# Weight preparation in a fused attention and MLP kernel: mixing pinned to a later place, splits without GpSimd, six evictions by ScalarE

## The chip, the cores and the metric

One core of one Trainium2 chip runs the whole program. The metric is the device time of one execution in microseconds (us), lower is better. A core has five engines with a queue of instructions each: TensorE (matmuls; loading weights overlaps them), VectorE, ScalarE, GpSimd and SyncE, which here only issues DMA transfers. An engine works through its queue in order: an instruction that waits holds up all that stand behind it.

## The reference

Sigmoid attention for 8 batches of 12 heads, 448 positions and 64 channels, then two matrix products with a bend between them:

```python
scores = scale * np.matmul(q, k.transpose(0, 1, 3, 2)) - np.log(S)
attn = 1.0 / (1.0 + np.exp(-scores))
x = (attn @ v), heads side by side        # 3584 x 768
h = x @ w_in                              # 768 x 2048
g = np.where(h >= 1, h, np.where(h <= -1, 0.0, (h + 1) ** 2 / 4))
out = g @ w_out                           # 2048 x 768
```

## The kernel before

**Numbers.** The weights arrive as 64-bit floats. `Weight.convert` turns each chunk of 128 rows (16 chunks for w_in, 16 for w_out) into float32: ScalarE takes the high words (L226), VectorE adds the low bits (L234, L235), one of the two finds the largest value. Once a group of 8 chunks is converted, `find_scale` (L251 and on) makes a power of two from its largest value, and `Weight.split` makes two half-precision tiles of each chunk: high (ScalarE, L266 or L270) and low, the rest (VectorE, L271, one instruction). For some chunks GpSimd makes the low tile with two instructions (L267, L268): for w_in those of chunks 8 to 15, asked for from the sixth chunk of batch 0's first product on (`POOL_FROM`), for w_out every sixth, chunks 1, 7 and 13 (`WOP`). The half-precision tiles of chunk f lie where the float32 values of chunk f - 1 lay, so the splits of a weight follow one another. Products of such pairs are three matmuls: high by high, high by low, low by high.

**Stages.** First comes batch 0's attention in float32, beside the conversion of w_in. Then batch 0's MLP: 48 units of its first product (`up`, L708, six matmuls of 448 columns to a unit, three units to a chunk of h), then 24 units of the first half of its second product (`downs(0, 0)`, L744: chunks 0 to 7 of w_out, evicted from PSUM by VectorE in L754 and stored to `part` in DRAM). Between the units stand the attention steps of batch 1 (30 steps to a batch, five to a pair of heads) and the conversion of w_out. Batch 1's MLP follows: 24 units of its first product, 24 of the second half of batch 0's second product (`downs(0, 1)`, evicted with `part` added in L750), 24 more of its first product, then 48 of its own second product: units 0 to 119. Attention steps of batch 2 are spread evenly over units 0 to 101 (`share`, `DW`); at unit 102 `start_blocks` and `finish_blocks` turn batch 2's attention into operands (L516 to L537).

From batch 2 on the first product is done with one level of Strassen-like blocks: seven products instead of eight (`up_blocks`, L674), which need sums and differences of blocks of w_in. `mix(i)` makes them for chunks i and i + 8, eight steps in all: VectorE adds the high and low tiles back together (two instructions in L618, tile `mixa`), forms four block sums (L622 to L625), ScalarE and VectorE split two rows of them (L631, L632, tile `mixs`), VectorE rescales the unmixed blocks (four instructions in L641, tile `mixp`), and SyncE stores both to `blocks` in DRAM (L635, L644), from where batches 2 to 7 load them as sets (L650). The three tiles of a step come from a pool of two buffers (`raww`), which w_out's raw words used before. The steps stand in the program at batch 1's units 8, 17, 27, 36, 46, 56, 65 and 75 (`MIX0`, `MIX1`).

The bend of a chunk of h (`bend`) is two instructions of ScalarE (L721, L724) and three of VectorE (L722, L723, L725); L721 and L723 read PSUM. An attention step writes scores to PSUM, ScalarE takes the sigmoid, and from pair 14 on its result is split into two half-precision tiles (ScalarE L451, VectorE L452).

**What sets the order.** The program is traced in the order of the Python code, and a planner with a model of the engines' times then orders each engine's queue: an instruction may be put ahead of earlier ones when its operands are ready in the model. `tc.keep_in_program_order(ins)` forbids this for one instruction: it is issued after the instruction traced just before it on the same engine. `tc.high_priority` raises priority. Semaphores are placed by the framework.

Of the kernel before, what the change touches and what calls it, by code (L numbers as in the profile page):

```python
# [18 lines left out]
AF = mybir.ActivationFunctionType  # L19
ALU = mybir.AluOpType  # L20
# [14 lines left out]
NA = 8  # L35
AHEAD = 2
# [5 lines left out]
B0 = 9  # L42
B1 = 66
GPOOL = 1
POOL_FROM = 6
SUMS = (), (0, 1, 2, 3, 4, 8, 9, 10, 11, 12)
BEHIND = (1, 3, 4, 6, 7, 8, 10, 12, 13, 14, 16, 18, 19, 21, 22, 24)
SUM_LAG = 4
# [5 lines left out]
SB = 2  # L54
QA = 17
QT = 3
WOP = 6
MIXP = 0
CORN = 10
TP = 1  # L60

DW = 8
MIX0 = 8
MIX1 = 85
Q_PRIO = 72

PM = 9
# [5 lines left out]
def sigmoid_attention_mlp(ctx: ExitStack, tc: tile.TileContext, first_qvk, qkv, w_in, w_out, out_t):  # L73
    nc = tc.nc
# [103 lines left out]
    class Weight:  # L178
# [79 lines left out]
            self.scale.append(s)  # L258
            self.inv.append(inv)

        def split(self, f, pool=False):
            if f >= NFC:
                return
            w, hi, lo, scale = self.f32(f), self.sb[:, f, 0, :], self.sb[:, f, 1, :], self.scale[f >= NA]
            if pool:
                nc.scalar.activation(hi, w, AF.Copy, scale=scale)  # L266
                nc.gpsimd.tensor_scalar(out=w, in0=w, scalar1=scale, scalar2=1.0, op0=ALU.mult, op1=ALU.mult)  # L267
                nc.gpsimd.tensor_tensor(out=lo, in0=w, in1=hi, op=ALU.subtract)  # L268
            else:
                nc.scalar.activation(hi, w, AF.Copy, scale=scale)  # L270
                nc.vector.scalar_tensor_tensor(  # L271
                    out=lo, in0=w, scalar=scale, in1=hi, op0=ALU.mult, op1=ALU.subtract
                )


    raws, maxes, ready, hls, sums = {}, {}, {}, {}, {}
# [335 lines left out]
    def mix(i):  # L612

        to, ratio, minus = mixed["to"], mixed["ratio"], mixed["minus"]
        f, g, H = i, i + NFC // 2, DM // 2
        a = raw_p.tile([P, 2 * DM], I32, tag="raww", name="mixa").bitcast(F32).rearrange("p (r n) -> p r n", r=2)
        for r, chunk in ((0, f), (1, g)):
            (nc.gpsimd if r < MIXP else nc.vector).tensor_tensor(  # L618
                out=a[:, r], in0=w_in_sb[:, chunk, 0, :], in1=w_in_sb[:, chunk, 1, :], op=ALU.add
            )  # L620
        a11, a12, a21, a22 = a[:, 0, :H], a[:, 0, H:], a[:, 1, :H], a[:, 1, H:]
        nc.vector.tensor_tensor(out=a22, in0=a21, in1=a22, op=ALU.add)  # L622
        nc.vector.scalar_tensor_tensor(out=a21, in0=a11, scalar=ratio, in1=a21, op0=ALU.mult, op1=ALU.subtract)
        nc.vector.scalar_tensor_tensor(out=a11, in0=a11, scalar=minus, in1=a22, op0=ALU.mult, op1=ALU.add)
        nc.vector.scalar_tensor_tensor(out=a12, in0=a12, scalar=ratio, in1=a11, op0=ALU.mult, op1=ALU.subtract)  # L625
        st = raw_p.tile([P, 2 * DM], I32, tag="raww", name="mixs").bitcast(F16)
        sv = st.rearrange("p (r t h n) -> p r t h n", r=2, t=2, h=2)
        for r in range(2):
            src = a[:, r].rearrange("p (t n) -> p t n", t=2)
            hi = sv[:, r, :, 0, :]  # L630
            nc.scalar.activation(hi, src, AF.Copy, scale=to[1])  # L631
            nc.vector.scalar_tensor_tensor(  # L632
                out=sv[:, r, :, 1, :], in0=src, scalar=to[1], in1=hi, op0=ALU.mult, op1=ALU.subtract
            )
        nc.sync.dma_start(out=blocks[i][:, 3 * DM :], in_=st)  # L635
        pl = raw_p.tile([P, 2 * DM], I32, tag="raww", name="mixp").bitcast(F16)[:, : 3 * DM]
        pv = pl.rearrange("p (t h n) -> p h t n", t=3, h=2)
        for t0, n, chunk, k in ((0, 2, f, 0), (2, 1, g, 1)):
            src = w_in_sb[:, chunk].rearrange("p h (t n) -> p h t n", t=2)[:, :, 2 - n :, :]
            for h in range(2):  # L640
                nc.vector.tensor_scalar(  # L641
                    out=pv[:, h, t0 : t0 + n, :], in0=src[:, h], scalar1=to[k], scalar2=None, op0=ALU.mult
                )
        nc.sync.dma_start(out=blocks[i][:, : 3 * DM], in_=pl)  # L644
# [84 lines left out]
    def down(b, m, u, k):  # L729

        lo, hi = (0, NFC) if k is None else (GROUPS[k].start, GROUPS[k].stop)
        if u == 0:
            hold["po"] = ps_mo.tile([P, 512], F32, tag="mo", name="po")
            hold["o"] = out_p.tile([P, S], F32, tag="o", name="o")
            if m == 0:
                hold["od"] = down_sc[b, k]()
            if k == 1:
                nc.sync.dma_start(out=hold["o"], in_=part[m])
        po, o = hold["po"], hold["o"]

        pair = (u, u + NFC // 2) if b >= SB else (lo + 2 * u, lo + 2 * u + 1)
        for f in pair:
            for wh, gh in ((0, 0), (0, 1), (1, 0)):
                nc.tensor.matmul(  # L744
                    po[:, :S], w_out_sb[:, f, wh, m * P : (m + 1) * P], ghl[:, f, gh, :],
                    start=f == lo and wh + gh == 0, stop=f == hi - 1 and wh == 1,
                )
        if u == (hi - lo) // 2 - 1:
            if k == 1:
                nc.vector.scalar_tensor_tensor(  # L750
                    out=o, in0=po[:, :S], scalar=hold["od"], in1=o, op0=ALU.mult, op1=ALU.add
                )
            else:
                nc.vector.tensor_scalar(out=o, in0=po[:, :S], scalar1=hold["od"], scalar2=None, op0=ALU.mult)  # L754
            dst = part[m] if k == 0 else out_t[m * P : (m + 1) * P, b * S : (b + 1) * S]
            nc.sync.dma_start(out=dst, in_=o)

# [87 lines left out]
    for u, unit in enumerate(units):  # L845
        while at < 2 * NPIECE and B0 + (at - NPIECE) * (B1 - B0) // NPIECE <= u:
            step(at)
            at += 1
        if wi.at < NFC + 1:
            convert(wi, NFC + 1)  # L850
            wi.find_scale()
            group_scales(0, inv_x, 1)
        f, r = divmod(u, NCC // 2)

        assert all(at >= NPC * (p + 1) or (f + 1) * S * 4 <= slot_of(p) * 3 * S * 4 for p in range(NP, NFULL)), u
        if r == 0 and f < NFC:
            wi.split(f + AHEAD, f >= POOL_FROM)
        if wo.at < NA + 1:
            convert(wo, min(NA + 1, (u + 1) * (NA + 1) // WO_A))
            if wo.at == NA + 1:  # L860
                wo.find_scale()
                split_at = 0
        elif wo.at < NFC + 1:
            convert(wo, min(NFC + 1, NA + 1 + (u + 1 - WO_A) * (NFC - NA) // (WO_B - WO_A)))
            if wo.at == NFC + 1:
                wo.find_scale()
                roots()
        if len(wo.scale):
            while split_at < min(NA, 2 * (u + 1 - WO_A)):
                wo.split(split_at, split_at % WOP == 1)  # L870
                split_at += 1
        unit()
    while at < 2 * NPIECE:
# [5 lines left out]
    for b in range(1, B):  # L879
        units = ups_blocks(b) + downs(b)  # L880
        last = len(units) - 96 + LAST
        if b == 1:
            mix_scales()
            units = ups(1, 0, NA) + downs(0, 1) + ups(1, NA, NFC) + downs(1)
            last = len(units) - LAST1
        first = at

        share = [DW if b < SB or u < len(units) - 48 else 8 for u in range(last)]
        share = [sum(share[:u]) / sum(share) for u in range(last + 1)]
        with ExitStack() as order:  # L890
            if b >= PM:
                order.enter_context(tc.manual_schedule(engines={mybir.EngineType.PE}))
            for u, unit in enumerate(units):
                while at < min(b + 2, B) * NPIECE and (at - first) < share[min(u + 1, last)] * NPIECE:
                    step(at)
                    at += 1
                if b == 1:
                    while split_at < min(NFC, NA + (u + 1) * (NFC - NA) // (NA * NCC // 2 - 2)):
                        wo.split(split_at, split_at % WOP == 1)
                        split_at += 1  # L900
                    while mixed_at < NFC // 2 and u >= MIX0 + mixed_at * (MIX1 - MIX0) // (NFC // 2):
                        mix(mixed_at)
                        mixed_at += 1
                if b + 1 < B and u == last:
                    begun = start_blocks()
                unit()
                if b + 1 < B and u == last:
                    inv_x = finish_blocks(*begun)
                    block_scales(b + 1, inv_x)
                if b == 1 and u == last - 2:  # L910
                    for n in range(3):
                        load_set(n)
# [39 lines left out]
```

## Time and profile before

| | us |
|---|---|
| median of 3 runs | 1179.65 |
| lowest, highest | 1177.72, 1180.30 |
| profiled execution | 1179.06 |
| its span, as the profile has it | 1177.3 |
| TensorE busy in the span | 1140.0 (97%) |
| VectorE busy | 826.9 (70%) |
| ScalarE busy | 699.9 (59%) |
| GpSimd busy | 321.1 (27%) |

The profile is of one execution. A row of the table by stretch gives, for a part of the span, the busy time and number of instructions of PE (TensorE's matmuls), PEld (its weight loads), DVE (VectorE), ACT (ScalarE) and POOL (GpSimd), then the clock that was granted to TensorE as a share of full speed, the DMA engines' share and GB/s. With a tile's name it counts the instructions of that tile alone. A row of the view of one source line gives the count, the shortest, median and longest duration in ns, and the first and last start in us. In the chain each row is a start, a time and what it was spent on. A wait is given as: who waited, for whom, us in total, times, longest. L618 is line 618 of the kernel. Busy time of TensorE is modelled from its pipeline, so "busy" means that matmuls were in flight.

### The profile page before, as it was taken

How to read it: one execution, taken by the hardware profiler on the slowest of the kernel's cores; microseconds unless marked ns; L12 is line 12 of the kernel's file. 1: busy time of each engine (PE TensorE's matmuls, PEld its weight loads, DVE VectorE, ACT ScalarE, POOL GpSimd, SP SyncE). 2: the span in 40 equal slices, each digit the busy share in tenths (PEclk: the TensorE clock that was granted, in tenths of full speed). 3: DMA queues.
4: the chain of work that ended last, by engine and by line, in shares of the span. 5: the costliest groups of instructions: out<-in, count | busy, mean ns of one | idle time of the engine just before them, and what ended most of it. 6: DMA issues, size and time to landing. Idle time of an engine off the chain costs nothing.

```text
span 1177.3 us, 20221 instructions
## 1 busy us (share of the span) xinstructions
PE 1140.0 (97%) x7662; PEld 668.5 (57%) x7662; DVE 826.9 (70%) x1758; ACT 699.9 (59%) x1162; POOL 321.1 (27%) x389
## 2 busy tenths in 40 slices
PE   8889988799999999999999999999999999999998
PEld 2234333344445786467854677457764677558954
DVE  6998997997935788368873689367873688736830
ACT  6986984675743686448764577546864486523410
POOL 0025010100341353425353236233533253310000
PEclk9999999999999999999999999999999999999999
DMA  9941643447421465215733166324652256302400
GB/s 358 376 164 62 207 134 138 154 159 245 160 67 55 142 201 204 72 57 166 262 131 92 57 229 200 126 64 143 205 198 67 62 166 213 118 25 101 151 16 32
DMA packets 58113, 170.01 MB, mean 144 GB/s; under 512 B 8608, under 2 KB 39840, under 8 KB 51872
## 3 DMA queue, kind: packets, MB, share of 16 engines
q1 hardware_dynamic: 56288, 159.29, 39.6%
q10 hardware_dynamic: 1728, 9.44, 2.3%
q8 instruction: 60, 0.98, 0.4%
q14 instruction: 37, 0.30, 0.1%
HBM read 126.94 MB, written 23.40 MB: 128 GB/s over the span
## 4 chain that ended last, share of the span: by engine, by line
PE 74%; DVE 6%; DMA 5%; ACT 1%; POOL 1%; issue 1%; SPq 0%; POOLq 0%; ACTq 0%
PE po L744 34%; PE ph L674 23%; PE pav L484 7%; PE psc L402 3%; PE ph L708 3%; PE psc L411 2%; DMA blocks<-mixs 2%; PE psc L397 2%; DMA w_in_sb<-blocks 1%; DVE mixs L632 1%; DMA raw<-qkv 1%; DMA blocks<-mixp 1%; DVE w_out_sb L271 1%; DVE mixa L618 1%; DMA w_out_sb<-w_out 0%
## 5 line engine op out<-in xcount | busy, mean ns | idle before, releaser
L744 PE MATMUL po<-ghl,w_out_sb 128*128 128x448 f16 x2304 | 446.2, 353 | 7.2 <-DVE w_out_sb L271 3.6
L744 PEld LDWEIGHTS <-w_out_sb 128*128 128x128 f16 x2304 | 222.2, 98 | 224.5 <-issue 13.5
L674 PE MATMUL ph<-w_in_sb 128*128 128x224 f16 x3024 | 307.7, 259 | 1.7 <-DMA w_in_sb<-blocks 1.3
L674 PEld LDWEIGHTS <-w_in_sb 128*128 128x128 f16 x3024 | 282.6, 98 | 30.6 <-issue 27.3
L452 DVE SCALAR_TENSOR_TENSOR ahl<-psc,ahl 128x896 f16<-128x896 f32 (+1 forms) x170 | 153.0, 900 | 112.4 <-ACT ahl L451 110.4
L443 ACT ACTIVATE psc<-psc,nls,sqk 128x896 f32<-128x896 f32 (+1 forms) x136 | 129.6, 974 | 114.9 <-PE psc L411 97.1
L364 POOL TENSOR_SCALAR raw<-raw,qkv_s 128x448 f32<-128x448 f32 (+1 forms) x93 | 70.8, 774 | 451.1 <-DVE qkv_i L138 352.1
L451 ACT ACTIVATE ahl<-psc 128x896 f16<-128x896 f32 (+1 forms) x170 | 127.1, 763 | 29.9 <-DVE ahl L452 28.8
L708 PE MATMUL ph<-xhl,w_in_sb 128*128 128x448 f16 x576 | 114.7, 357 | 3.4 <-DVE g L723 2.0
L328 ACT ACTIVATE dump<-raw 128x448 f16<-128x448 f32 (+1 forms) x105 | 62.0, 590 | 77.6 <-DMA raw<-qkv 76.7
L683 DVE TENSOR_TENSOR xhl<-ph,xhl 128x224 f32<-128x224 f32 x240 | 87.8, 383 | 26.0 <-PE ph L674 19.8
L484 PE MATMUL pav<-ahl,v 128*64 128x448 f16 x748 | 96.5, 362 | 0.0
L721 ACT ACTIVATE g<-xhl,hr,ihr 128x448 f32<-128x448 f32 x96 | 69.0, 755 | 43.2 <-DVE xhl L683 42.3
L724 ACT ACTIVATE ghl<-g 128x448 f16<-128x448 f32 x128 | 72.8, 574 | 35.5 <-DVE g L723 35.2
L725 DVE TENSOR_TENSOR ghl<-g,ghl 128x448 f16<-128x448 f32 x128 | 86.8, 686 | 7.9 <-ACT ghl L724 6.6
L708 PEld LDWEIGHTS <-w_in_sb 128*128 128x128 f16 x576 | 55.6, 99 | 64.1 <-issue 16.2
L722 DVE SCALAR_TENSOR_TENSOR g<-g,rk 128x448 f32<-128x448 f32 x112 | 81.8, 745 | 10.6 <-ACT g L721 10.4
L754 DVE TENSOR_SCALAR o<-po,od 128x448 f32<-128x448 f32 x48 | 32.5, 679 | 62.5 <-PE po L744 62.4
L402 PE MATMUL psc<-qk 128*128 128x448 f16 x252 | 66.3, 354 | 7.2 <-ACT a L440 3.6
L366 POOL TENSOR_TENSOR hl<-raw,hl 128x448 f16<-128x448 f32 x62 | 69.6, 1140 | 0.0
L723 DVE SCALAR_TENSOR_TENSOR g<-xhl,ihs,g 128x448 f32<-128x448 f32 x96 | 65.8, 703 | 0.3
L484 PEld LDWEIGHTS <-v 128*64 128x64 f16 x748 | 36.6, 109 | 38.7 <-issue 24.3
(156 smaller groups left out, 1142.5 us busy)
## 6 DMA issues: line engine op xcount, KB each, us to landing
w_in_sb<-blocks SPq DMA_DIRECT2D x48, 1344.0 KB, 6.5
raw<-qkv SPq DMA_DIRECT2D x34, 704.0 KB, 4.8
qk<-hl SPq DMA_DIRECT2D x320, 56.0 KB, 2.0
w_out_sb<-w_in SPq DMA_DIRECT2D x16, 768.0 KB, 11.1
out_t<-o SPq DMA_DIRECT2D x48, 224.0 KB, 1.9
blocks<-mixs SPq DMA_DIRECT2D x8, 768.0 KB, 3.6
w_out_sb<-w_out ACTq DMA_DIRECT2D x6, 768.0 KB, 5.0
raww<-w_out ACTq DMA_DIRECT2D x6, 768.0 KB, 5.0
```

Source lines behind the costliest of these rows:

```text
L402: nc.tensor.matmul(out, kq[:, j, 1, w], kq[:, j, 0, :], start=True, stop=False)
L443: nc.scalar.activation(a, a, AF.Sigmoid, bias=nls, scale=sqk)
L451: nc.scalar.activation(hi, x, AF.Copy, scale=ATT)
L452: nc.vector.scalar_tensor_tensor(out=lo, in0=x, scalar=ATT, in1=hi, op0=ALU.mult, op1=ALU.subtract)
L484: nc.tensor.matmul(pav[j * D : (j + 1) * D, :S], *terms[j][t], start=c == 0 and t == 0, stop=mid and t == len(terms[j]) - 1,)
L674: nc.tensor.matmul(out, w[:, wt, wh, c * P : (c + 1) * P], xc[:, xt, c, xh, :], start=j in (0, 2) and c + wh + xh == 0, stop=c == HC - 1 a ...
L683: add = lambda out, q, other: nc.vector.tensor_tensor(out=out, in0=quarter(q), in1=other, op=ALU.add)
L708: nc.tensor.matmul(ph[:, :S], w_in_sb[:, f, wh, c * P : (c + 1) * P], xhl[:, c, xh, :], start=c == 0 and wh + xh == 0, stop=c == NCC - 1 a ...
L722: nc.vector.scalar_tensor_tensor(out=g, in0=g, scalar=rt, in1=g, op0=ALU.min, op1=ALU.mult)
L724: nc.scalar.activation(hi, g, AF.Copy)
L725: (nc.gpsimd if f % GPOOL else nc.vector).tensor_tensor(out=ghl[:, f, 1, :], in0=g, in1=hi, op=ALU.subtract)
L744: nc.tensor.matmul(po[:, :S], w_out_sb[:, f, wh, m * P : (m + 1) * P], ghl[:, f, gh, :], start=f == lo and wh + gh == 0, stop=f == hi - 1 ...
```

## The change

1. `mix`: the two additions of L618 are pinned with `keep_in_program_order`, and the eight steps stand at batch 1's units 24, 33, 42, 51, 60, 69, 78 and 87. Nothing else of a step changes.
2. `share`: in batch 1 the first 24 units weigh half of the others when batch 2's attention steps are spread.
3. `split`: the branch for GpSimd is gone; all low tiles are made by VectorE in one instruction.
4. `down`: the six evictions of batch 0's first half of the second product (`k == 0`) are ScalarE's instead of VectorE's.

```diff
-POOL_FROM = 6
...
-WOP = 6
-MIXP = 0
...
-MIX0 = 8
-MIX1 = 85
+MIX0 = 24
+MIX1 = 96
...
-        def split(self, f, pool=False):
+        def split(self, f):
...
-            if pool:
-                nc.scalar.activation(hi, w, AF.Copy, scale=scale)
-                nc.gpsimd.tensor_scalar(out=w, in0=w, scalar1=scale, scalar2=1.0, op0=ALU.mult, op1=ALU.mult)
-                nc.gpsimd.tensor_tensor(out=lo, in0=w, in1=hi, op=ALU.subtract)
-            else:
-                nc.scalar.activation(hi, w, AF.Copy, scale=scale)
-                nc.vector.scalar_tensor_tensor(
-                    out=lo, in0=w, scalar=scale, in1=hi, op0=ALU.mult, op1=ALU.subtract
-                )
+            nc.scalar.activation(hi, w, AF.Copy, scale=scale)
+            nc.vector.scalar_tensor_tensor(out=lo, in0=w, scalar=scale, in1=hi, op0=ALU.mult, op1=ALU.subtract)
...
         for r, chunk in ((0, f), (1, g)):
-            (nc.gpsimd if r < MIXP else nc.vector).tensor_tensor(
+            tc.keep_in_program_order(nc.vector.tensor_tensor(
                 out=a[:, r], in0=w_in_sb[:, chunk, 0, :], in1=w_in_sb[:, chunk, 1, :], op=ALU.add
-            )
+            ))
...
-                nc.vector.tensor_scalar(out=o, in0=po[:, :S], scalar1=hold["od"], scalar2=None, op0=ALU.mult)
+                if k == 0:
+                    nc.scalar.activation(o, po[:, :S], AF.Copy, scale=hold["od"])
+                else:
+                    nc.vector.tensor_scalar(out=o, in0=po[:, :S], scalar1=hold["od"], scalar2=None, op0=ALU.mult)
...
-            wi.split(f + AHEAD, f >= POOL_FROM)
+            wi.split(f + AHEAD)
...
-                wo.split(split_at, split_at % WOP == 1)
+                wo.split(split_at)
...
-        share = [DW if b < SB or u < len(units) - 48 else 8 for u in range(last)]
+        share = [DW // 2 if b < SB and u < NA * NCC // 2 else DW for u in range(last)]
```

More of the change, by code (lines that the diff above doesn't have):

```diff
@@ L898, in sigmoid_attention_mlp @@
                     while split_at < min(NFC, NA + (u + 1) * (NFC - NA) // (NA * NCC // 2 - 2)):
-                        wo.split(split_at, split_at % WOP == 1)
+                        wo.split(split_at)
                         split_at += 1
```

## The prediction, made before the change was run

> **What bounds the kernel now.** I read the table of busy time by stretch first, then the table in slices of 10 us, then the chain of work that ended last, then VectorE's timeline and the waits. In the first table the columns are TensorE, its weight loads, VectorE, ScalarE and GpSimd (busy us, instructions), then TensorE's granted clock, the DMA share and GB/s.
>
> ```profile
> 80.00:140.00 60.00, 60.00 (x307) 26.36 (x304) 52.79 (x74) 44.04 (x73) 22.67 (x17) 1.00 0.33 113
> 140.00:160.00 20.00, 17.35 (x89) 6.78 (x89) 19.95 (x41) 16.25 (x25) 3.12 (x2) 1.00 0.59 189
> 160.00:190.00 30.00, 24.58 (x114) 8.44 (x111) 23.87 (x44) 22.23 (x40) 2.90 (x2) 0.94 0.29 87
> 190.00:230.00 40.00, 32.47 (x166) 15.16 (x166) 36.19 (x96) 20.85 (x29) 3.30 (x2) 0.99 0.45 155
> 230.00:247.00 17.00, 17.00 (x85) 8.22 (x84) 17.00 (x35) 11.84 (x21) 1.33 (x3) 0.93 0.62 210
> 247.00:358.00 111.00, 109.06 (x610) 52.81 (x609) 79.92 (x149) 64.71 (x106) 29.43 (x39) 0.98 0.48 153
> 358.00:386.00 28.00, 28.00 (x157) 14.33 (x156) 12.68 (x45) 8.80 (x15) 1.00 (x1) 1.00 0.09 33
> 386.00:1177.30 791.30, 784.96 (x5867) 516.81 (x5865) 519.03 (x1143) 445.81 (x768) 255.70 (x318) 1.00 0.38 130
> ```
>
> From 386 us on TensorE is busy 784.96 of 791.30 us; nothing that the change touches lies there. Between 80 and 140 us it is busy throughout. What can be won lies between 140 and 358 us. TensorE's idle time there is 2.65 us (140 to 160), 5.42 (160 to 190), 7.53 (190 to 230), none (230 to 247) and 1.94 (247 to 358): 17.5 us, while VectorE is busy 97.0 of the 107 us from 140 to 247. Besides idle time there is the clock:
>
> ```profile
> 180.00:190.00 10.00, 6.61 (x24) 1.87 (x23) 9.18 (x14) 5.23 (x11) 2.90 (x2) 0.83 0.01 4
> 220.00:230.00 10.00, 6.61 (x32) 2.52 (x31) 10.00 (x19) 7.74 (x11) 3.30 (x2) 0.95 0.10 40
> 230.00:240.00 10.00, 10.00 (x48) 4.89 (x47) 10.00 (x22) 6.65 (x12) 1.03 (x2) 0.88 0.70 255
> 300.00:310.00 10.00, 9.59 (x46) 4.22 (x46) 9.53 (x22) 8.98 (x17) 6.44 (x8) 0.83 0.71 225
> ```
>
> Three times the granted clock falls: 0.83 over 10 us is 1.7 us lost, 0.95 and 0.88 together 1.7, the last 0.83 again 1.7. The first two drops lie in or right behind slices in which TensorE stood idle 3.39 us. So 17.5 + 5.1 = 22.6 us is all that this part of the kernel can give.
>
> Who holds TensorE up is told by the chain (start, us, engine and line) and by VectorE's timeline:
>
> ```profile
> 158.10 1.73 DVE mixa L618 x2
> ...
> 172.40 8.37 DMA blocks<-mixs
> 180.79 1.83 DVE mixa L618 x2
> ...
> 206.06 7.08 DMA blocks<-mixs
> ...
> 228.91 15.46 PE ph L708 x72
> ...
> 249.34 2.84 PE po L744 x15
> ```
>
> ```profile
> 173.69 1.01 DVE L271 SCALAR_TENSOR_TENSOR w_out_sb<-w_out_sb,wo_s 128x768 f16<-128x768 f32 x1
> 180.79 1.83 DVE L618 TENSOR_TENSOR mixa<-w_in_sb 128x768 f32<-128x768 f16 x2 [6.09 <-DMA blocks<-mixs]
> ```
>
> ```profile
> 209.82 0.10 PEld L708 LDWEIGHTS <-w_in_sb 128*128 128x128 f16 x1 [0.20 <-issue]
> ```
>
> Batch 1's first product begins at 209.82, and the program places the first mixing step eight units behind that; yet it runs at 158.10, inside batch 0's second product. The planner has pulled it ahead. A mixing step's first addition then stands in VectorE's queue for a buffer that a store still reads: 6.09 us at 180.79. Behind it in the same queue wait the splits of w_out (L271) for which TensorE is waiting. That is the chain's own path until 228.91, where TensorE takes over.
>
> **The change, part by part.** *Mixing leaves the stretch before 247 us.* How much VectorE time it has, by stretch, for the two groups of tiles it writes (mixa with mixs, then mixp):
>
> ```profile
> 140.00:247.00 107.00, 31.65 (x39) 9.22 (x10) 0.97 0.46 151
> 247.00:358.00 111.00, 19.90 (x25) 5.62 (x6) 0.98 0.48 153
> ```
>
> ```profile
> 140.00:247.00 107.00, 4.79 (x16) 0.97 0.46 151
> 247.00:358.00 111.00, 4.98 (x16) 0.98 0.48 153
> ```
>
> 31.65 + 4.79 = 36.4 us of VectorE's 97.0 go from the first stretch, and the waits at L618 with them. Unit 24 of batch 1, the new place of the first step, is where the chain turns from L708 to L744, at 249.34. The pin ties L618 behind the VectorE instruction traced just before it, which there is a bend of batch 1 or an attention piece and can't run early. What stays: all of the 2.65 us before 160 (the first step starts only at 158.10); of the 5.42 us to 190 I keep 1.4, because a split of w_out overwrites the place of the one before, so that ScalarE's and VectorE's halves (VectorE's is 1.007 us, below) alternate, slower than the matmuls that use them; of the 7.53 us to 230 I keep 2.5 for the chain of batch 1's scales, which no part of the change shortens. Removed: 4.0 + 5.0 = 9.0 us, and with them two drops of the clock, 3.4 us: 12.4 us. Bounds: about 6 (half of it, if the chains keep it) and 16.4 (all idle time and both drops).
>
> *Splits from GpSimd to VectorE and ScalarE.*
>
> ```profile
> L722 DVE SCALAR_TENSOR_TENSOR g<-g,ru x7: 673/1991/2128, 84.8 to 105.7; 128x448 f32<-128x448 f32 x7
> ```
>
> ```profile
> L722 DVE SCALAR_TENSOR_TENSOR g<-g,ru x7: 671/678/685, 112.2 to 142.8; 128x448 f32<-128x448 f32 x7
> ```
>
> ```profile
> L271 DVE SCALAR_TENSOR_TENSOR w_out_sb<-w_out_sb,wo_s x13: 1002/1007/1022, 148.5 to 236.2; 128x768 f16<-128x768 f32 x13
> ```
>
> Eight splits of w_in come to VectorE: 8 x 1.007 = 8.1 us. But the first row of L722 is taken while GpSimd splits, the second when it no longer does: the same instruction has a median of 1.991 against 0.678 us. Seven times 1.31 is 9.2 us that VectorE gets back, so the net is -1.1 us. Three splits of w_out add 3.0 us, with a like relief that I count at nothing. The Trainium skill, Perfetto Trace Analysis, section Optimizing Scalar/DVE Operations, advises giving work of a saturated VectorE to ScalarE or even GpSimd, and that speaks against this edit; by it alone VectorE would get 11 us more here. Its page SBUF — State Buffer, section Who interferes with whom, says that a VectorE instruction with two SBUF inputs is fully blocked while a GpSimd instruction that reads SBUF holds the shared port; the two L722 rows agree with the second rule. Either way TensorE is busy 60.00 of 60.00 us here and hides it: price nothing, from -1 to, with that cover gone, +8 us of delay for w_out's conversion behind it.
>
> *ScalarE evicts batch 0's half product.*
>
> ```profile
> L754 DVE TENSOR_SCALAR o<-po,od x6: 670/676/683, 190.0 to 205.2; 128x448 f32<-128x448 f32 x6
> ```
>
> ```profile
> L493 ACT ACTIVATE x<-pav,sqk x34: 616/630/653, 280.1 to 1046.6; 128x448 f32<-128x448 f32 x34
> ```
>
> VectorE loses 6 x 0.676 = 4.1 us, ScalarE gets about 6 x 0.630 = 3.8 us, in a stretch where it is busy 20.85 of 40 us. Behind each such wait on ScalarE's queue stand batch 1's sigmoids, splits and xhl; I price it at nothing, between -1 and +2 us.
>
> *What comes later.* From unit 24 to unit 102, where batch 2's scales begin (L516), VectorE now has 79.92 us in 111, of which 19.90 + 4.98 are mixing. All eight steps together are 31.65 + 19.90 + 4.79 + 4.98 = 61.3 us, so it will have 79.92 - 24.9 + 61.3 = 116.3. The new shares give the first 24 units 4 attention steps of 30 instead of 7 (96 of 720 against 24 of 102), so three more come later:
>
> ```profile
> L452 DVE SCALAR_TENSOR_TENSOR ahl<-psc,ahl 128x896 f16<-128x896 f32 (+1 forms) x22 | 20.1, 918 | 14.8 <-ACT ahl L451 14.5
> ```
>
> ```profile
> L516 DVE TENSOR_REDUCE xm<-xm x1: 143/143/143, 358.2 to 358.2; 128x1 f32<-128x6 f32 x1
> ```
>
> Three pieces at 0.918 are 2.8 us: 119.1. TensorE's own work in the stretch is 111 - 1.94 idle - 1.7 clock = 107.4 us (and the moved steps' matmuls, which leave the earlier stretch). VectorE is over by at most 11.7 us. Add its waits for the stores:
>
> ```profile
> DVE mixa L618 <- DMA blocks<-mixs: 9.7, 4, 6.1
> ```
>
> ```profile
> L635 SPq DMA_DIRECT2D blocks<-mixs x8: 319/322/452, 172.4 to 302.0; - x8
> ```
>
> The sixteen stores move past SyncE's attention copies, 0.32 us an issue, 5 us in 111; that is small, but a store was on the chain for 7 to 8 us, so the next step's L618 can still stand waiting, with bends, evictions and attention pieces queued behind it and TensorE waiting for their PSUM banks. I take the same 9.7 us again: 11.7 + 9.7 = 21.4. Against it stands slack:
>
> ```profile
> L534 DVE SCALAR_TENSOR_TENSOR w_in_sb<-x,x_s,w_in_sb x3: 912/919/921, 366.1 to 371.4; 128x672 f16<-128x672 f32 x3
> ```
>
> ```profile
> L674 PE MATMUL ph<-w_in_sb x108: 259/259/269, 385.9 to 398.8; 128*128 128x224 f16 x108
> ```
>
> Batch 2's operands are ready at 371.4 + 0.9 = 372.3 and used at 385.9: 13.6 us. What shows on TensorE is 21.4 - 13.6 = 7.8 us, in place of the 1.94 + 1.7 = 3.6 there now: 4.2 us dearer.
>
> **Sum.** -12.4 + 4.2 = -8.2 us. The profiled execution took 1179.06 us, which gives 1170.9; the median of the runs shown is 0.6 us above it, so 1171.5.
>
> **The rivals.** *TensorE stays the bound throughout.* VectorE's backlog drains under batch 1's last product, where it is busy 12.68 of 28 us, and nothing shows: -12.4 - 3.6 = -16.0, so 1163.6. For it: 13.6 us of slack and waits that mixing might fill (14.8 us of idle time before L452). Against it: 119.1 us of work in 107.4.
>
> *VectorE becomes the bound of batch 1 (slower).* Three steps, at units 51, 60 and 69, fall among batch 1's bends, whose PSUM banks only VectorE frees. If TensorE stalls there, the slack at the end is of no use and the whole 21.4 us shows: -12.4 - 3.6 + 21.4 = +5.4, so 1185.1. It decides once the stalls behind 247 us exceed 12.4 + 3.6 = 16.0 us.
>
> *The change doesn't do what it says, or gives back as much as it takes.* A pin only orders L618 behind one instruction; were that one early, mixing would still run before 210 us. Or the stalls come to 16 us. Either is 1179.7.
>
> **How the numbers follow.** Forecast 0.50 (its own range 1166 to 1177), TensorE the bound 0.22, VectorE the bound 0.17, no net effect 0.11. The range 1162 to 1183 takes in the forecast, most of the first rival, the last one, and the near part of the slower one; about 0.2 is left out. A measurement of this kernel can tell about 0.2%, 2.4 us. Faster by more: 0.50 + 0.22 and a little of the last case, 0.73; within: 0.10; slower: 0.17.
>
> **What would show it.** Right: the first L618 behind batch 1's unit 23, so none before 220 us; batch 1's first L708 some 8 to 12 us before 209.82; L722 near 0.68 us between 85 and 106 us; TensorE idle under 4 us from 160 to 230; VectorE over 95% busy in the hundred microseconds behind unit 24. Wrong: stalls of TensorE from 140 to 230 as before without mixing there (then the chains of w_out and of the scales were the cause, and mixing only stood beside them); batch 2's first L674 later than 385.9; a clock drop in batch 1's bends.

## The result, and the profile after

The changed kernel takes 1166.33 us (median of 4 runs, 1164.44 to 1167.94) against 1179.75 us for the kernel before (4 runs): a ratio of 0.9889, 95% interval 0.9870 to 0.9908, 13.4 us. Timed again later, the same kernel gave 0.9901 (0.9886 to 0.9915). The profiled execution took 1165.96 us with a span of 1164.2, 13.1 us under the span before.

The table by stretch for the kernel after (busy TensorE, weight loads, VectorE, ScalarE, GpSimd, then granted clock, DMA share, GB/s):

```profile
80.00:140.00 60.00, 60.00 (x302) 25.64 (x300) 48.42 (x82) 44.73 (x73) 0.56 (x2) 1.00 0.33 113
140.00:160.00 20.00, 18.99 (x99) 7.21 (x98) 18.59 (x45) 16.73 (x26) 0.00 (x0) 1.00 0.60 189
160.00:190.00 30.00, 30.00 (x156) 12.78 (x154) 12.73 (x27) 21.48 (x41) 0.00 (x0) 1.00 0.25 77
190.00:230.00 40.00, 38.82 (x206) 18.70 (x205) 32.60 (x83) 26.97 (x40) 1.77 (x2) 1.00 0.28 79
230.00:330.00 100.00, 97.71 (x542) 46.98 (x541) 92.35 (x162) 62.99 (x106) 21.94 (x26) 0.98 0.47 164
330.00:372.00 42.00, 39.82 (x219) 19.51 (x218) 37.55 (x83) 19.42 (x30) 13.57 (x13) 1.00 0.58 202
372.00:1164.20 792.20, 785.27 (x5866) 516.64 (x5864) 518.33 (x1143) 444.85 (x768) 254.72 (x318) 1.00 0.38 130
```

TensorE's idle time from 140 to 230 us has gone from 15.60 to 1.01 + 0 + 1.18 = 2.19 us, and the two drops of the clock with it. From 160 to 190 us VectorE is busy 12.73 of 30 us where it was 23.87. Behind 230 us TensorE now stands idle for 2.29 + 2.18 = 4.47 us (1.94 before), with VectorE busy 92.35 of 100. From 372 us on, the kernel is as it was within 1 us.

The first row is the mixing's additions (count, shortest, median and longest ns, first and last start), the next two are batch 2's last operands and its first matmuls; then, in the chain, batch 1's first product:

```profile
L608 DVE TENSOR_TENSOR mixa<-w_in_sb x16: 941/952/1785, 233.6 to 350.2; 128x768 f32<-128x768 f16 x16
```

```profile
L524 DVE SCALAR_TENSOR_TENSOR w_in_sb<-x,x_s,w_in_sb x3: 906/910/918, 360.3 to 366.3; 128x672 f16<-128x672 f32 x3
```

```profile
L664 PE MATMUL ph<-w_in_sb x207: 259/259/270, 371.7 to 399.6; 128*128 128x224 f16 x104
```

```profile
198.66 10.40 PE ph L698 x54
```

(L608 was L618, L698 was L708, and so on: the lines of `mix` and what follows it moved up by 7 to 10.) Mixing starts at 233.6 instead of 158.0 us and ends about 359 instead of 304. Batch 1's first product starts at 198.6 instead of 209.8, batch 2's at 371.7 instead of 385.9: 14.2 us earlier. Of the 13.6 us between the last operand and its use, 371.7 - 367.2 = 4.5 us are left.

VectorE's time for mixing, by tile, in the kernel after:

```profile
230.00:358.00 128.00, 53.13 (x64) 14.92 (x16) 0.99 0.48 168
```

```profile
230.00:358.00 128.00, 14.33 (x29) 0.99 0.48 168
358.00:372.00 14.00, 0.91 (x4) 1.00 0.72 241
```

53.13 + 14.33 + 0.91 = 68.4 us, where the same instructions took 61.3 us before. The 7 us come from the neighbourhood. The four rescalings of a step still take 1.20 us in five of the eight steps, but 4.07, 2.53 and 2.62 us in the three that fall beside GpSimd's scaling and splitting of q, k and v; the two additions of a step take 3.02 and 2.25 us instead of 1.82 in two steps beside GpSimd. What that leads to is seen at the two largest stalls of TensorE. From the timeline of all engines around 297 us:

```profile
290.83 1.40 DVE L622 SCALAR_TENSOR_TENSOR mixs<-mixa,mixes,mixs 128x768 f16<-128x768 f32 x1 [0.34 <-ACT mixs L621]
...
293.16 4.07 DVE L631 TENSOR_SCALAR mixp<-w_in_sb,mixes 128x768 f16<-128x768 f16 x4
...
293.74 2.24 POOL L356 TENSOR_TENSOR hl<-raw,hl 128x448 f16<-128x448 f32 x2
...
300.02 1.28 PE L387 MATMUL psc<-hl,w_in_sb 128*128 128x448 f16 x3 [2.29 <-DVE ahl L442]
```

The four rescalings take 4.07 us here, against 1.20 us in the steps of the kernel before; the attention piece that TensorE waits for (L442) stands behind them. Around 350 us it is the diagonal of batch 2's scale, which stands behind the last step's additions (VectorE, then TensorE):

```profile
348.97 0.14 DVE L506 TENSOR_REDUCE xm<-xm 128x1 f32<-128x6 f32 x1
349.04 2.25 DVE L608 TENSOR_TENSOR mixa<-w_in_sb 128x768 f32<-128x768 f16 x2
351.21 0.28 DVE L161 TENSOR_SCALAR diag<-ident,xm 128x128 bf16<-128x128 bf16 x1
```

```profile
351.55 0.23 PE L171 MATMUL psc<-diag,one 128*128 128x128 bf16 x1 [1.33 <-DVE diag L161]
```

### The profile page after: what moved, and what is told of

It is laid out like the page before. It is cut to its first block, busy times and chain, and to the rows that moved or that the text cites. A ratio compares the mean times of both kernels' runs of the same rounds, so it can differ in the third digit from the quotient of the medians.

```text
span 1164.2 us, 20204 instructions
## 1 busy us (share of the span) xinstructions
PE 1137.7 (98%) x7662; PEld 667.4 (57%) x7662; DVE 826.7 (71%) x1763; ACT 702.6 (60%) x1168; POOL 293.2 (25%) x367
## 4 chain that ended last, share of the span: by engine, by line
PE 76%; DVE 8%; ACT 5%; DMA 5%; POOL 2%; issue 2%; SPq 1%; POOLq 0%; ACTq 0%; DVEq 0%
PE po L734 30%; PE ph L664 23%; PE pav L474 8%; PE ph L698 7%; PE psc L392 3%; PE psc L401 3%; DMA raw<-qkv 2%; PE psc L387 1%; DVE ahl L442 1%; ACT a L430 1%; ACT psc L433 1%; DMA w_out_sb<-w_in 1%; DVE mixa L608 1%; ACT dump L318 1%; DVE mixp L631 1%
## 5 line engine op out<-in xcount | busy, mean ns | idle before, releaser
L442 DVE SCALAR_TENSOR_TENSOR ahl<-psc,ahl 128x896 f16<-128x896 f32 (+1 forms) x170 | 152.8, 899 | 97.8 <-ACT ahl L441 95.8
L698 PE MATMUL ph<-xhl,w_in_sb 128*128 128x448 f16 x576 | 112.7, 353 | 0.0
L715 DVE TENSOR_TENSOR ghl<-g,ghl 128x448 f16<-128x448 f32 x128 | 83.8, 661 | 8.8 <-ACT ghl L714 8.3
L698 PEld LDWEIGHTS <-w_in_sb 128*128 128x128 f16 x576 | 54.6, 98 | 57.9 <-issue 9.1
L712 DVE SCALAR_TENSOR_TENSOR g<-g,rk 128x448 f32<-128x448 f32 x112 | 78.9, 720 | 12.0 <-ACT g L711 11.7
L413 POOL COPY w_in_sb<-hl 64x128 f16<-64x128 f16 x68 | 33.4, 490 | 163.5 <-DVE hl L350 161.5
L356 POOL TENSOR_TENSOR hl<-raw,hl 128x448 f16<-128x448 f32 x62 | 72.0, 1182 | 0.0
L747 DVE TENSOR_SCALAR o<-po,od 128x448 f32<-128x448 f32 x42 | 28.5, 678 | 51.8 <-PE po L734 51.8
```

What stands on the lines that cost most here:

```text
L442: nc.vector.scalar_tensor_tensor(out=lo, in0=x, scalar=ATT, in1=hi, op0=ALU.mult, op1=ALU.subtract)
L698: nc.tensor.matmul(ph[:, :S], w_in_sb[:, f, wh, c * P : (c + 1) * P], xhl[:, c, xh, :], start=c == 0 and wh + xh == 0, stop=c == NCC - 1 a ...
L712: nc.vector.scalar_tensor_tensor(out=g, in0=g, scalar=rt, in1=g, op0=ALU.min, op1=ALU.mult)
L715: (nc.gpsimd if f % GPOOL else nc.vector).tensor_tensor(out=ghl[:, f, 1, :], in0=g, in1=hi, op=ALU.subtract)
```

## The experiments

The experiments were timed in three groups, each beside the kernel before, whose medians were 1177.44 us (mixing alone to even shares), 1178.15 (no pin, pin at the old place, thin mixing, rescaling by ScalarE) and 1177.10 (the other four). Ratios are against those.

**Mixing alone, on the kernel before.**

```diff
-MIX0 = 8
-MIX1 = 85
+MIX0 = 24
+MIX1 = 96
...
-            (nc.gpsimd if r < MIXP else nc.vector).tensor_tensor(
+            tc.keep_in_program_order(nc.vector.tensor_tensor(
```

> The kernel before with the first part of the change alone: the two additions of a mixing step pinned, the steps at units 24 to 87. Theory A (mixing in VectorE's queue between 158 and 229 us is what held TensorE up): 1167 to 1171 us, the first product of batch 1 begins near 199 us, and TensorE's idle time from 160 to 230 us falls from 12.9 us to under 4. Theory B (the relief of VectorE by the ended GpSimd splits and the six evictions is what counts): 1176 to 1180 us and idle time of 9 us or more.

Measured: 1172.71 us, ratio 0.9961 (0.9946 to 0.9976). By time this lies between the two theories, 4.7 us of gain. The profiled execution took 1169.43 us, one of the two shortest of nine, so it can show less than the median lost. The profile says where:

```profile
160.00:190.00 30.00, 30.00 (x153) 11.90 (x152) 15.16 (x37) 19.21 (x36) 2.55 (x2) 1.00 0.24 71
190.00:230.00 40.00, 38.03 (x201) 18.02 (x199) 31.07 (x77) 27.27 (x43) 3.86 (x4) 1.00 0.28 83
230.00:330.00 100.00, 98.80 (x556) 47.97 (x554) 89.67 (x158) 60.06 (x97) 21.91 (x26) 1.00 0.47 156
330.00:376.00 46.00, 40.34 (x211) 19.44 (x211) 40.33 (x88) 19.85 (x33) 13.13 (x13) 0.96 0.57 201
```

In the early stretch theory A holds: 1.97 us idle from 160 to 230 instead of 12.95. But TensorE is idle for 5.66 us from 330 to 376, with a drop of the clock.

**All parts but mixing** (the kernel after with no pin and units 8 to 75).

> The kernel after with its mixing as before (no pin, units 8 to 75), all other parts of the change kept. Theory A: 1176 to 1181 us, a mixing step again before 170 us. Theory B: 1166 to 1170 us.

Measured: 1174.27 us, ratio 0.9975 (0.9960 to 0.9989). Mixing is back at 159.0 us, and TensorE is idle again for 2.54 + 8.19 us from 160 to 230:

```profile
160.00:190.00 30.00, 27.46 (x137) 10.51 (x134) 23.64 (x40) 20.36 (x31) 0.00 (x0) 1.00 0.34 117
190.00:230.00 40.00, 31.81 (x157) 14.40 (x155) 37.06 (x100) 28.60 (x47) 0.00 (x0) 0.91 0.46 168
```

Theory B falls; A's lower bound of 1176 is missed by 1.7 us, as the other parts bring 2.9 us of themselves. Mixing alone gives 0.39%, the rest alone 0.25%, both together 1.0 to 1.1%: they help each other.

**Splits by GpSimd again** (`f >= 6` of w_in, every sixth of w_out).

> The kernel after with the low tiles of chunks 8 to 15 of w_in and 1, 7 and 13 of w_out made by GpSimd again, as before. Theory A: 1165 to 1168 us, as the stretch from 80 to 140 us has TensorE busy throughout; the first bend instruction with both inputs in SBUF again takes about 2.0 instead of 0.68 us while GpSimd splits. Theory B: 1170 us or more.

Measured: 1167.02 us, ratio 0.9917 (0.9900 to 0.9933), within the measurement of the kernel after. The bend instruction is back at a mean of 1.66 us while GpSimd splits (0.68 in the kernel after), and it costs TensorE nothing there; where the splits of w_out begin, TensorE is idle for 2.60 us against 1.01:

```profile
140.00:160.00 20.00, 17.40 (x91) 7.17 (x91) 19.97 (x44) 16.47 (x26) 3.12 (x2) 1.00 0.58 190
```

```profile
L719 DVE SCALAR_TENSOR_TENSOR g<-g,ru 128x448 f32<-128x448 f32 x8 | 13.2, 1662 | 1.1 <-ACT g L718 1.1
```

Two things are slower in that stretch with GpSimd's split of chunk 1. The next split's high half on ScalarE waits 1.97 us for it, since the splits follow one another; and VectorE's instructions beside it take longer, a conversion of w_out 1.44 instead of 0.95 us and a cast of two columns 1.60 instead of 0.16. Which of the two costs TensorE the 1.6 us was not separated.

**Attention of batch 2 spread evenly again.**

```diff
-        share = [DW // 2 if b < SB and u < NA * NCC // 2 else DW for u in range(last)]
+        share = [DW for u in range(last)]
```

> The kernel after with batch 2's attention steps spread evenly again over batch 1's units. Theory A: 1165 to 1169 us: three attention steps come earlier, VectorE has room before unit 24 now that no mixing is there, and it is less full behind it. The rival, that the shares carry part of the gain, gives 1170 us or more, with stalls of TensorE before unit 24.

Measured: 1168.37 us, ratio 0.9927 (0.9911 to 0.9943), 3.1 to 4.5 us over the kernel after by ratio, which was timed in other groups, with intervals that just overlap or just don't. There are no more stalls before unit 24, so the rival's reason is wrong; the loss is at the other end, 5.60 us idle against 2.18, where the wait for the diagonal is 3.61 instead of 1.33 us and the clock drops:

```profile
330.00:375.00 45.00, 39.40 (x212) 19.15 (x210) 38.94 (x87) 19.14 (x31) 13.12 (x13) 0.96 0.58 206
```

```profile
352.61 0.29 PE L171 MATMUL psc<-diag,one 128*128 128x128 bf16 x1 [3.61 <-DVE diag L161]
```

Mixing alone shows the same loss, and it too has even shares. So the shares seem to matter once mixing is late, and would then be most of how the parts help each other; late mixing and new shares without the other two parts were not run.

**No pin, new place.**

> The kernel after without the pin, the steps still at units 24 to 87 of the program. If the planner's freedom is what put mixing early: the first mixing addition again before 200 us and 1172 to 1180 us. If the place in the program is enough: the first addition at 225 us or later and 1165 to 1168 us.

Measured: 1174.59 us, ratio 0.9965 (0.9953 to 0.9977). The planner pulls the first step to 157.5 us again:

```profile
L608 DVE TENSOR_TENSOR mixa<-w_in_sb x16: 942/951/1032, 157.5 to 278.8; 128x768 f32<-128x768 f16 x16
```

The place in the program does nothing without the pin: this kernel and the one with mixing as before agree within the measurement.

**Pin, old place** (units 8 to 75).

> The kernel after with the pin, but the steps at the old units 8 to 75. If it is the pin that counts (no mixing inside batch 0's second product): 1166 to 1170 us, with some stalls between 200 and 230 us as splits of w_out and mixing meet. If the place counts as much: 1172 us or more.

Measured: 1172.07 us, ratio 0.9948 (0.9932 to 0.9963), at the edge of the second case. The first addition stands directly behind a split of w_out and runs at 196.55 us, 1.7 us before batch 1's first product and not eight units behind its start: the pin holds it behind VectorE's work, not behind TensorE's. TensorE is busy throughout from 160 to 190 us, but stands idle for 7.35 us behind that, most of it in one wait for a bend:

```profile
190.00:230.00 40.00, 32.65 (x165) 15.13 (x164) 38.10 (x93) 25.10 (x36) 0.00 (x0) 0.91 0.31 107
```

```profile
218.38 3.89 PE L698 MATMUL ph<-xhl,w_in_sb 128*128 128x448 f16 x13 [6.19 <-DVE g L713]
```

```profile
212.21 1.81 DVE L608 TENSOR_TENSOR mixa<-w_in_sb 128x768 f32<-128x768 f16 x2
213.94 1.01 DVE L263 SCALAR_TENSOR_TENSOR w_out_sb<-w_out_sb,wo_s 128x768 f16<-128x768 f32 x1
214.87 1.87 DVE L712 SCALAR_TENSOR_TENSOR g<-g,rk 128x448 f32<-128x448 f32 x3
```

No store is waited for here. VectorE works through scales, splits of w_out and mixing before it comes to the bend that frees TensorE's PSUM bank. So of what mixing brings (0.25% without it, 0.52% here, 1.0 to 1.1% in the kernel after) the pin at the old place gives about a third, and the new place, which is nothing without the pin, the rest.

**Thin mixing, on the kernel before.**

```diff
-        nc.vector.tensor_tensor(out=a22, in0=a21, in1=a22, op=ALU.add)
...
-            nc.vector.scalar_tensor_tensor(
-                out=sv[:, r, :, 1, :], in0=src, scalar=to[1], in1=hi, op0=ALU.mult, op1=ALU.subtract
-            )
+            nc.scalar.activation(sv[:, r, :, 1, :], src, AF.Copy, scale=to[1])
```

> The kernel before with thin mixing steps: the four block sums are left out and ScalarE makes the low half of mixs, so that a step takes about 3.2 instead of 7.7 us of VectorE, while its early place, its buffers, its stores and its waits stay; part of the mixing is not computed. If the time that mixing takes of VectorE is what held TensorE up: 1168 to 1173 us. If it is the wait of its first addition for the store at the head of VectorE's queue: 1176 us or more, with waits of 7 us or more at that line.

Measured: 1178.24 us, ratio 1.0003 (0.9994 to 1.0012): no change. VectorE's mixing from 140 to 247 us fell from 36.4 to 12.97 + 8.41 = 21.4 us (rows: mixa, then mixp), ScalarE's rose from 9.22 to 23.97, and the wait for the store stayed:

```profile
140.00:247.00 107.00, 12.97 (x14) 23.97 (x28) 0.95 0.51 171
```

```profile
140.00:247.00 107.00, 8.41 (x28) 0.95 0.51 171
```

```profile
DVE mixa L618 <- DMA blocks<-mixs: 10.0, 3, 4.7
```

By the expectation on record this speaks for the wait. But ScalarE makes half of every split of w_out too, so part of the work only changed queues, and with lighter steps the planner starts seven of them before 247 us instead of five. What the trace does show is that the wait reaches TensorE: its longest idle time here, 4.69 us, ends with the operand of batch 1's first product (L508), which stands in VectorE's queue behind an addition that waited 3.09 us for a store.

```profile
212.77 0.96 DVE L618 TENSOR_TENSOR mixa<-w_in_sb 128x768 f32<-128x768 f16 x1 [3.09 <-DMA blocks<-mixs]
```

```profile
216.36 12.61 PE L702 MATMUL ph<-xhl,w_in_sb 128*128 128x448 f16 x51 [4.69 <-DVE xhl L508]
```

**Stores that don't hold the buffers, on the kernel before.**

```diff
-        nc.sync.dma_start(out=blocks[i][:, 3 * DM :], in_=st)
+        other = w_in_sb[:, f : f + 2].rearrange("p s h n -> p (s h n)")
+        tc.keep_in_program_order(nc.sync.dma_start(out=blocks[i][:, 3 * DM :], in_=other))
...
-        nc.sync.dma_start(out=blocks[i][:, : 3 * DM], in_=pl)
+        tc.keep_in_program_order(nc.sync.dma_start(out=blocks[i][:, : 3 * DM], in_=other[:, : 3 * DM]))
```

> The kernel before, where the stores of a mixing step have the same number, size and queue but take their data from w_in's chunks instead of the mixed tiles, so that no mixing buffer waits for a store; what batches 2 to 7 load is then not the mixed weights. VectorE's mixing work and its early place stay. If the wait for the store at the head of VectorE's queue is what counted: 1168 to 1173 us on the scale of 1179 for the kernel before (6 to 11 us faster), no wait for a store at the first addition. If mixing's time on VectorE counts: within 3 us of the kernel before, or slower.

Measured: 1184.28 us, ratio 1.0060 (1.0045 to 1.0075): slower. Mixing waits for no store any more, and TensorE is idle from 160 to 247 us for 6.38 + 7.45 + 5.30 us, where it was 5.42 + 7.53 + 0:

```profile
160.00:190.00 30.00, 23.62 (x111) 8.26 (x110) 28.76 (x52) 21.37 (x38) 3.66 (x2) 0.96 0.14 42
190.00:230.00 40.00, 32.55 (x159) 14.87 (x158) 37.59 (x93) 21.55 (x29) 2.55 (x2) 0.93 0.23 74
230.00:247.00 17.00, 11.70 (x54) 5.69 (x54) 16.94 (x37) 10.87 (x20) 0.72 (x2) 0.74 0.08 18
```

```profile
234.87 0.16 PE L158 MATMUL pm<-mb,one 128*128 128x3 bf16 x1 [8.35 <-DVE g L724]
```

With the wait gone VectorE fills its time with mixing (28.76 of 30 us busy instead of 23.87) and seven steps instead of five start before 247 us. The longest wait, 8.35 us for a bend, ends a stretch in which VectorE never pauses: parts of two mixing steps, splits of w_out and scales stand ahead of that bend. So the wait for the store is not needed for the loss; it even spaced the steps out. Nor is it harmless, as the thin run shows. The cause is mixing in the queues ahead of work that TensorE needs, whether it waits there or works. How much each of the two costs in the kernel before, and whether ScalarE's part counts as well, is left open.

**Rescaling by ScalarE, on the kernel after** (tile mixp).

```diff
-                nc.vector.tensor_scalar(
-                    out=pv[:, h, t0 : t0 + n, :], in0=src[:, h], scalar1=to[k], scalar2=None, op0=ALU.mult
-                )
+                nc.scalar.activation(pv[:, h, t0 : t0 + n, :], src[:, h], AF.Copy, scale=to[k])
```

> The kernel after with the four rescalings of a mixing step (tile mixp) on ScalarE instead of VectorE. VectorE loses about 10 us between 230 and 360 us, where it is over 93% busy, ScalarE gains about 24 us, where it is some 55% busy. If VectorE is what makes the stalls left there (6 us): 1161 to 1165 us. If they are chains of waits: 1165 to 1168 us, or more where ScalarE's queue holds up sigmoids.

Measured: 1167.15 us, ratio 0.9908 (0.9893 to 0.9923): no gain. The stall at 297 us shrinks from 2.29 to 0.79 us, that at the diagonal grows from 1.33 to 2.17 us, and the mixing's first additions now wait 6.8 us for stores in all. Relief of VectorE alone, 92.35 to 85.43 us in 100, is not what the rest hangs on.

```profile
230.00:330.00 100.00, 98.78 (x545) 46.42 (x544) 85.43 (x140) 75.11 (x125) 22.74 (x26) 1.00 0.47 160
```

**Evictions by VectorE again.**

> The kernel after with the six evictions of batch 0's half product on VectorE again. With mixing out of that stretch VectorE is busy under 8 of 10 us from 170 to 200 us, so theory A gives no more than 1 us over the kernel after of the same call. If the evictions carry a part of the gain: 3 us or more.

Measured: 1166.57 us, ratio 0.9915 (0.9900 to 0.9929), against 1165.74 and 0.9901 (0.9886 to 0.9915) for the kernel after in the same group. The difference is not told apart from none; the profile shows 0.30 + 1.92 us idle from 160 to 230 us against 1.18.

**Mixing four units earlier** (units 20 to 79).

> The kernel after with the mixing steps four units earlier at the start and ten at the end (units 20 to 79). The last step's additions then stand about 25 instructions ahead of batch 2's diagonal in VectorE's queue instead of right before it. If the stall at 350 us (1.5 us and a drop of the clock in some runs) comes from that neighbourhood: 1 to 3 us faster than the kernel after of the same call. If VectorE's total work behind unit 24 decides: the same within 1 us.

Measured: 1166.04 us, ratio 0.9906 (0.9892 to 0.9921): the same as the kernel after. The last step stands eight units earlier (79 for 87, not ten) and did run earlier, yet the wait for the diagonal was still 1.06 us, and a new one of 0.79 us came at 221 us. The neighbourhood of the last step was not the point.

**The kernel after once more.**

> The kernel after itself once more, on the same chip as the others of this call, as the measure for them: 0.987 to 0.991 of the kernel before.

Measured: 1165.74 us, ratio 0.9901 (0.9886 to 0.9915). No version beat it.

## Why the prediction was right, point by point

The sign, the place and most of the mechanism held: 1166.3 us lies in the range and at the lower edge of the forecast's own. The signs of being right came as written but for the last: first addition at 233.6 us, batch 1's first product 11.2 us earlier, bends at a median of 0.680 us in the stretch of the splits,

```profile
L712 DVE SCALAR_TENSOR_TENSOR g<-g,ru x7: 676/680/685, 84.9 to 103.4; 128x448 f32<-128x448 f32 x7
```

1.18 us of idle time from 160 to 230, batch 2 earlier. VectorE behind unit 24 was busy 92%, not over 95%. Of the signs of being wrong one came too, a drop of the clock in batch 1's bends (0.83 from 300 to 310 us); it was badly chosen, as it stood in the kernel before as well.

*The first term, -12.4 us, was too small.* It came out at 15.60 - 2.19 = 13.4 us of idle time and 3.4 us of clock: -16.8, just past the bound of 16.4 that I had given. The step that failed is what I kept: 1.4 us for the chain of w_out's splits and 2.5 for the chain of batch 1's scales. With mixing out of the queues the first is nothing; behind it 1.18 us of idle time are left, and they are waits for sigmoids of batch 1's attention (ScalarE, L430), not for the scales. Nor were the 2.65 us before 160 us fixed: they fell to 1.01, and with GpSimd's splits back they are 2.60. I had priced the splits at nothing. From 80 to 140 us that is right for TensorE, though VectorE got back more than I thought: its busy time there fell by 4.4 us (52.79 to 48.42) where I had 1.1. The first of the three w_out splits was the exception. The Trainium skill, SBUF — State Buffer, section Who interferes with whom, says that a VectorE instruction with two SBUF inputs contends with a GpSimd instruction that reads SBUF; the conversion of w_out, which has two, agrees with 1.44 against 0.95 us. The advice that I set against this part, in the Trainium skill, Perfetto Trace Analysis, section Optimizing Scalar/DVE Operations, goes on to say that moving work between VectorE and GpSimd might not help, as the two share a port; so it did not speak against the edit, and the run with GpSimd's splits, which is no faster, agrees.

*The second term, +4.2 us, was too large*, by 1.7: idle time behind 230 us is 4.47 instead of 1.94, with one drop of the clock in each, so +2.5. The account behind it (VectorE over by 11.7 us, 9.7 us of waits, 13.6 us of slack) had the right shape and wrong entries. The waits for stores hardly came back (1.5 us), but mixing itself became 7 us dearer beside GpSimd, and 9.1 of the 13.6 us of slack were used up.

*The sum* is -16.8 + 2.5 = -14.3, against 14.2 us measured at batch 2's start; 1 us of it is lost behind. Both terms were off in the same direction, so no error hid another, and 1166.3 lies nearer to the first rival's 1163.6 than to the forecast's 1171.5. That rival, TensorE the bound throughout, is not what happened either: 4.47 us of idle time and one drop of the clock are left behind 230 us, where it had none.

*The reason given for the first term was half wrong.* I named the wait for the store at the head of VectorE's queue and the mixing work together, "the chain's own path". The run without those waits was slower, so it was not the wait by itself. *The other rivals:* "VectorE becomes the bound of batch 1" did not come, though its sign, a stall among the bends with a clock drop, is there once (2.3 us at 297). That a pin might not hold did not come at units 24 to 87; at the old place it came in part, with the first addition at 196.55 us. Without the pin the change would have given a third. What I did not see is that parts of the change need one another: the shares, which I treated as a cost of 2.8 us, seem to be worth 3 to 4 us once mixing is late. Why TensorE waits 2.3 us longer for the diagonal with even shares was not settled.

## What to carry to other kernels

Where a planner orders the queues, look up when background work really runs; here it began 50 us ahead of the product in whose midst it was written, in front of what TensorE waited for, and moving its place in the program did nothing until the two additions of a step were pinned. A wait on the chain isn't yet the whole cause: taking the wait away let more of the same work in and cost 7 us. Work moved to a free stretch is priced by the neighbours that it gets there, so look at what GpSimd does in that stretch.

## What the runs showed of the hardware

A VectorE rescaling from half precision to half precision, one SBUF input and a scalar, is slowed by GpSimd as one with two inputs is: four of them took 4.07 us beside GpSimd's subtractions and 1.20 us without. The Trainium skill, SBUF — State Buffer, section Who interferes with whom, counts this form among those that can take the shared port; the trace agrees. The additions of L608 took 2.25 us at 349 us, beside GpSimd's work for batch 2, against 1.83 us at 180.79 in the kernel before, where GpSimd stood idle. At 247.89 us it was the other way round: the additions kept their 1.82 us, and GpSimd's two copies beside them took 2.82 us, against 1.06 at 265.41 us.

An idle stretch of TensorE under 3 us does not always cost the clock: about 2.3 us at 297 us brought a drop to 0.83 of full speed over the next 10 us in the kernel after, but in the run with GpSimd's splits 2.89 us idle between 300 and 310 us, 2.47 of them in one wait, brought none. The kernel after, then the run with the splits:

```profile
290.00:300.00 10.00, 7.74 (x43) 3.73 (x42) 9.66 (x15) 6.34 (x9) 7.95 (x11) 1.00 0.48 171
300.00:310.00 10.00, 9.97 (x49) 4.64 (x49) 9.94 (x16) 7.54 (x15) 0.00 (x0) 0.83 0.61 225
```

```profile
300.00:310.00 10.00, 7.11 (x42) 3.60 (x42) 10.00 (x15) 6.25 (x11) 0.15 (x1) 1.00 0.81 292
```
